# Merging and joining block inverses in one step, with decays and Gram matrices one step further ahead

## The chip, the cores and the metric

The kernel runs on one core of one Trainium2 chip. The metric is the device time of one execution in microseconds (us). TensorE (PE), VectorE (DVE), ScalarE (ACT) and GpSimd (POOL) compute, each working off its own list of instructions in order; SyncE (SP) issues the DMAs of this kernel, also in order.

## The reference

Three stages follow each other: a recurrent attention over 768 time steps for 4 batches and 8 heads with a state of 40x40, a feed-forward layer with a convolution of three taps, and a mixing layer with Fourier transforms, a norm and two matrices. The change touches the first:

```python
for t in range(S):
    kt, vt, rt = (k[:, :, t], v[:, :, t], r[:, :, t])
    wt, at, bt = (w[:, :, t], a[:, :, t], b[:, :, t])
    y[:, :, t] = np.einsum('bhd,bhde->bhe', rt, state)
    Sa = np.einsum('bhde,bhe->bhd', state, at)
    state_decay = state * wt[:, :, None, :] - np.einsum('bhd,bhe->bhde', Sa, bt)
    state = state_decay + np.einsum('bhd,bhe->bhde', vt, kt)
...
h = np.maximum(x @ w_in, 0.0)
...
gate = 1.0 / (1.0 + np.exp(-conv_out))
return (h * gate @ w_out).astype(np.float32)
```

## The kernel before, in words

The recurrence is done in 12 chunks of 64 time steps. Inside a chunk it is a triangular system, so that each chunk needs the inverse of a 64x64 triangular matrix per head and batch. `Attn.run` (L583 and on) counts steps n from 0 to 51; step n works on chunk n // 4 and batch n % 4, in stages: `stage_u` applies the inverse, `stage_h` (3 steps later, for the next chunk), `stage_s` and `stage_g` (1 step later), `stage_y` (2 steps later), `stage_sb` and `stage_o` (3 steps later). `stage_g` ends in one DVE product that writes the tile `gt` (L470); there is one in each step, so that the ends of two of them in a row bound a step on DVE.

Work is done ahead in `ahead` (L578). For a half chunk (two batches) `load_pre` (L146) loads `w`, `a` and `kb` and `decay` (L153) makes the decays: two scans on DVE (L161 and L165), and on POOL the products with `kb` (L176) and `a` (L168). This leads by LD = 17 steps. `gram` (L205) leads by LG = 15: matmuls of `abd` and `kb`, copies on ACT into `l0`, `l1` (tile `l`, L234 to L236) and `lk`.

Two chunks form a group (the first two chunks stand alone), and `inverse` (L312) inverts a group's diagonal blocks at once: a transpose of `l0` into A on DVE (L313), then 30 pairs of DVE instructions, a product (L333) and a sum (L336), each pair depending on the one before: the chain. POOL then clears a triangle (L338, L340), DVE makes three transposes (L343 into `t`, L346 twice into `tt`). The merge is a set of small matmuls on PE (`bp`), copied by ACT to `t` (L364); the join a second set (`mp`), copied to `tt` (L377). `stage_u` of the group's first chunk reads `tt`; the step in which it does so is the group's `end` (8, 16, 24, 32, 40 for the groups of two chunks).

The chain's instructions are given out at a rate over the steps between a group's start and its end (`rate`, L665 or so, in `run`), and `joins` (L516) issues the merge in step end - 2 and the join in step end - 1:

```python
for last, m in (("merge", v["end"] - 2), ("join", v["end"] - 1)):
    if v["last"] == last and n >= m:
```

A group starts when the Gram matrices of both its chunks have been issued (`na + LG >= 8 * g`), which is in step end - 7. A scheduler then puts the instructions of each engine into their final order. Between the steps runs the side work (`Moe.prep`): pieces of the later layers' weights are read as pairs of words and turned into floats by `unpack` (L766): ACT writes `pm` (L775) and the low words `py` (L776), DVE works on `pm` (L778, L780, L785), POOL adds `py` (L782), DVE and ACT split off a low part (L749, L752). The 33 last pieces are unpacked during the feed-forward layer, 64 unpackings in all with the one of the convolution's weights.

Of the kernel before, what the change touches and what calls it, by code (L numbers as in the profile page):

```python
# [10 lines left out]
F32 = mybir.dt.float32  # L11
# [13 lines left out]
P3 = HG * D  # L25
# [28 lines left out]
PC = 256  # L54
# [9 lines left out]
RI = 0.8  # L64
SIDE = 0.75
N1ST = 4
NA = 7
HL = 3
LG = 15
LD = 17  # L70
ST0 = 29
ST2 = 1
WARM = 4
# [25 lines left out]
class Attn:  # L99
# [53 lines left out]
    def decay(self, c, hb):  # L153
        nc, pre = self.nc, self.pre
        d = self.hf[c, hb]
        w, a, kb = d["w"], d["a"], d["kb"]

        wx = pre.tile([P3, 6, 66], F32, name="wx", tag="wx", bufs=11)
        vx = self.early.tile([P3, 6, 66], F32, name="vx", tag="vx", bufs=2)
        flat = [v.rearrange("p a b -> p (a b)") for v in (w, wx, vx)]  # L160
        nc.vector.tensor_tensor_scan(flat[2][:, ::-1], flat[0][:, ::-1], self.ends[:, ::-1], 0.0,  # L161
                                     op0=ALU.mult, op1=ALU.add)

        nc.vector.reciprocal(self.ends.rearrange("p (a b) -> p a b", b=66)[:, :, 0:1], vx[:, :, 1:2])
        nc.vector.tensor_tensor_scan(flat[1], flat[0], self.ends, 0.0, op0=ALU.mult, op1=ALU.add)  # L165
        nc.gpsimd.tensor_copy(wx[:, :, 65:66], vx[:, :, 1:2])
        e = nc.vector if c < 1 else nc.gpsimd
        e.tensor_tensor(a, a, wx[:, :, 0:C], op=ALU.mult)  # L168
        for h in range(HG):
            if c < 1:  # L170
                mul = nc.vector.tensor_scalar_mul if h == 2 else nc.scalar.mul
                v = mul(self.abd[hb][:, h], a, self.mdiag[:, D * h:D * h + 1])
                self.late = self.late if h == 2 else v
            else:
                nc.sync.dma_start(self.abd[hb][D * h:D * h + D, h], a[D * h:D * h + D])
        self.markp = nc.gpsimd.tensor_tensor(kb, kb, vx[:, :, 2:66].unsqueeze(2).to_broadcast([P3, 6, 2, C]), op=ALU.mult)  # L176
        d.update(wx=wx, vx=vx)
# [337 lines left out]

    def joins(self, live, n):  # L516
        for v in live:
            for last, m in (("merge", v["end"] - 2), ("join", v["end"] - 1)):
                if v["last"] == last and n >= m:
                    v["last"] = next(v["inv"], None)  # L520
                    yield
                    break

    def step(self, n, pre):
        def at(k):
            return divmod(n - k, B) if 0 <= n - k < B * NCH else (None, None)

# [15 lines left out]
        if c is not None:  # L546
            self.stage_g(c, b)
            if b % 2 and c + 1 < NCH:
                self.load_z(c + 1, b // 2)
            yield  # L550
        for _ in pre:
            yield
        c, b = at(3)
# [8 lines left out]
        if c is not None:  # L562
            self.stage_o(c, b)
            yield


    def in_range(self, flag):
# [10 lines left out]
    def ahead(self, n):  # L578
        m = n + LD
        if m % 2 == 0 and m < B * NCH:  # L580
# [4 lines left out]
            yield  # L585
        m = n + LG
        if m < B * NCH:
# [6 lines left out]
    def run(self, side):  # L594
# [24 lines left out]
        inv = self.inverse(0)  # L619
# [35 lines left out]
        live, g = [], 1  # L655
# [9 lines left out]
        for n in range(B * NCH + 4):  # L665
# [3 lines left out]
            while g <= NCH // 2 and na + LG >= 8 * g and len(live) < 2:  # L669
                end = 8 * g - 8 if g > 1 else 4  # L670
# [4 lines left out]
            pre = []  # L675
            for _ in range(1 + (n < NA)):
                if na <= n:
                    pre.append(self.ahead(na))
                    na += 1
            for _ in self.step(n, itertools.chain(self.joins(live, n), *pre)):  # L680
                sd += SIDE if n >= N1ST else 0.0
                while sd > 0:
                    with ExitStack() as st:
# [29 lines left out]
class Moe:  # L713
# [54 lines left out]
    def unpack(self, tp, raw, p, w):  # L768
        nc = self.nc

        def t(tag, dt):
            return tp.tile([128, PC], dt, name=tag, tag=tag, bufs=2)[:p, :w]
        lo, hi = raw[:, :, 0], raw[:, :, 1]
        m, y = t("pm", F32), t("py", I32)
        nc.scalar.activation(m, hi.bitcast(F32), AF.Abs)  # L775
# [3 lines left out]
        m = m.bitcast(I32)  # L779
# [630 lines left out]
```

## Time and profile before

| what | value |
|---|---|
| median of 3 runs | 1005.81 us (1003.6 to 1008.03) |
| the profiled execution | 1006.97 us |
| its span, first to last instruction | 1005.0 us |
| mean granted TensorE clock | 0.908 |
| stretch of the recurrence's steps 4 to 47, by the ends of `gt` | 119.54 to 503.36 us |

The profile gives the busy time of each engine, the waits (who stood idle, and whose instruction ended the wait), the busy times in chosen stretches, and the instructions in order of time. A wait by PE for a DVE instruction means that PE, which works in order, stood still with all that stands behind in its list. A busy time of DVE near the length of a stretch means that DVE sets the pace there. Share of busy time over the whole span says little, since the three stages have different limits.

### The profile page before, as it was taken

Reading aid. Unit: us, or ns where it says so; the run is one execution under the profiler, and the core shown is the slowest. Engines: PE = TensorE matmul, PEld = TensorE weight load, DVE = VectorE, ACT = ScalarE, POOL = GpSimd, SP = SyncE. Lnnn points to the kernel's source line nnn. Section 1 sums busy time; section 2 is a strip of 40 time slices with the busy share of each in tenths; the row PEclk is TensorE's granted clock in tenths of the full one; section 3 lists DMA queues with packets and bytes.
Section 4 is the critical chain, followed back from the end, with each engine's and each line's share of the span. In section 5 each row is a group of like instructions: output and inputs, shape, how many; then the busy total and the mean of one; then the engine's idle time right before and its main releaser. Section 6 shows DMA issues by size and latency. Waiting matters only on the chain. (4 is left out here: it accounts for less than half of the span.)

```text
span 1005.0 us, 21806 instructions
## 1 busy us (share of the span) xinstructions
PE 824.0 (82%) x8178; PEld 748.7 (75%) x8178; DVE 670.5 (67%) x1320; ACT 518.4 (52%) x1448; POOL 437.7 (44%) x507
## 2 busy tenths in 40 slices
PE   5548749747866868859699799998999999999997
PEld 3447638736766767849587577776879999999997
DVE  6994895994996894983169787978694444424321
ACT  4656638745865766535265566657464431222211
POOL 5455345653564553443157666765563112101000
PEclk8758768987997997978799999999999999999999
DMA  9623344662662752637545452212105000000000
GB/s 233 173 64 96 92 122 134 179 185 75 173 173 73 194 135 77 165 82 198 133 129 133 160 171 88 90 47 60 53 1 171 21 1 21 20 20 21 20 14 31
DMA packets 102989, 101.15 MB, mean 101 GB/s; under 512 B 47272, under 2 KB 89115, under 8 KB 102875
## 3 DMA queue, kind: packets, MB, share of 16 engines
q1 hardware_dynamic: 100907, 94.73, 33.5%
q0 software_dynamic: 1968, 4.93, 1.5%
q8 instruction: 67, 1.10, 0.5%
q14 instruction: 47, 0.39, 0.1%
HBM read 74.81 MB, written 20.76 MB: 95 GB/s over the span
## 5 line engine op out<-in xcount | busy, mean ns | idle before, releaser
L878 DVE SCALAR_TENSOR_TENSOR c<-h,cw,c 128x384 f32<-128x384 f32 x128 | 111.5, 875 | 21.5 <-ACT c L876 17.9
L1132 DVE SCALAR_TENSOR_TENSOR gl<-hp,gh 128x384 fp32r<-128x384 f32 x80 | 44.4, 556 | 111.3 <-ACT gh L1131 111.3
L895 PE MATMUL acc<-w_out_f,z 128*128 128x320 f32 x384 | 114.8, 436 | 4.7 <-POOL z L882 2.0
L1131 ACT ACTIVATE gh<-hp 128x384 fp32r<-128x384 f32 x80 | 39.2, 491 | 149.9 <-PE hp L701 149.7
L895 PEld LDWEIGHTS acc<-w_out_f,z 128*128 128x128 f32 x384 | 71.3, 190 | 28.2 <-POOL z L882 3.4
L701 PE MATMUL hp<-xh,w_in_h 128*128 128x386 f32 x192 | 76.1, 396 | 15.5 <-ACT h L869 15.5
L701 PE MATMUL hp<-uh,w_ch_h 128*128 128x384 f32 x240 | 82.3, 343 | 0.0
L701 PE MATMUL hp<-ul,w_ch_h 128*128 128x384 f32 x240 | 81.0, 338 | 0.0
L219 PE MATMUL gram<-abd,kb 120*128 120x192 f32 (+1 forms) x288 | 63.8, 371 | 16.9 <-DMA abd<-a 10.9
L1155 POOL DMA_INDIRECT out<-o,rows x12 | 11.8, 982 | 150.4 <-DVE o L1150 131.9
L457 POOL TENSOR_TENSOR st<-st,sm 120x360 f32<-120x360 f32 x40 | 43.5, 1087 | 70.8 <-DVE sm L456 47.8
L1145 PE MATMUL acc<-w_ch_h,gh 128*128 128x320 f32 x240 | 73.2, 312 | 0.0
L1145 PE MATMUL acc<-w_ch_l,gh 128*128 128x320 f32 x240 | 73.0, 309 | 0.0
L219 PEld LDWEIGHTS gram<-abd,kb 120*128 120x128 f32 x288 | 58.3, 235 | 19.0 <-issue 11.3
L388 PE MATMUL yp<-x,gt 128*64 128x40 f32 x768 | 63.6, 240 | 7.9 <-DVE gt L470 7.2
L333 DVE TENSOR_TENSOR tmp<-A 128x30 f32<-128x30 f32 (+9 forms) x150 | 68.1, 454 | 3.0
L388 PE MATMUL gp<-rbd,zt 120*128 120x192 f32 (+1 forms) x288 | 57.8, 341 | 13.4 <-DVE xo L509 6.0
L701 PE MATMUL hp<-xl,w_in_h 128*128 128x386 f32 x192 | 66.8, 348 | 0.0
L336 DVE TENSOR_TENSOR A<-A,tmp 128x30 f32<-128x30 f32 (+9 forms) x150 | 64.9, 433 | 2.6
L388 PE MATMUL bp<-t,l 32*32 32x32 f32 x768 | 21.2, 233 | 55.4 <-DVE t L343 50.8
L388 PEld LDWEIGHTS yp<-x,gt 128*64 128x64 f32 x768 | 58.5, 144 | 10.8 <-DVE gt L470 10.4
L879 ACT ACTIVATE c<-c 128x384 f32<-128x384 f32 x64 | 33.4, 521 | 61.0 <-DVE c L878 60.8
(225 smaller groups left out, 2610.9 us busy)
## 6 DMA issues: line engine op xcount, KB each, us to landing
kb<-in_kb SPq DMA_DIRECT2D x24, 360.0 KB
vbd<-in_vbd SPq DMA_DIRECT2D x24, 320.0 KB
xd<-xo SPq DMA_DIRECT2D x56, 90.0 KB
w<-in_w SPq DMA_DIRECT2D x24, 185.6 KB
a<-in_a SPq DMA_DIRECT2D x24, 180.0 KB
z<-in_zv SPq DMA_DIRECT2D x24, 180.0 KB
zt<-in_vt SPq DMA_DIRECT2D x24, 180.0 KB
rbd<-in_r SPq DMA_DIRECT2D x72, 60.0 KB
```

The lines of the kernel that those rows point to most:

```text
L219: nc.tensor.matmul(gp[:, 192 * gi:192 * gi + 64 * nh], d["kb"][:, bl * NG + gi].rearrange("p a b -> p (a b)"), abd[:, 0:nh, bl * NG + gi], ...
L333: nc.vector.tensor_tensor(tmp, A[:, s + 1:32, s:s + 1].to_broadcast([128, n, s]), A[:, s:s + 1, 0:s].to_broadcast([128, n, s]), op=ALU.mult)
L336: nc.vector.tensor_tensor(A[:, s + 1:32, 0:s], A[:, s + 1:32, 0:s], tmp, op=ALU.add)
L388: self.lastpe = op(*args, **kw)
L457: nc.gpsimd.tensor_tensor(self.st[b], self.st[b], t, op=ALU.add)
L701: nc.tensor.matmul(out, l, r, start=(j == 0), stop=(j == len(ops) - 1))
L878: nc.vector.scalar_tensor_tensor(c, h[:, j:HS + j], cw[:, f, j:j + 1], c, op0=ALU.mult, op1=ALU.add)
L879: nc.scalar.activation(c, c, AF.Sigmoid)
L895: nc.tensor.matmul(self.acc[t][:, 0:DM], z[:, ts], w[:, f], start=(f == 0), stop=(f == NF1 - 1))
L1131: self.mark = nc.scalar.activation(gh, hp[:, 0:HS], AF.Relu)
L1132: nc.vector.scalar_tensor_tensor(gl, hp[:, 0:HS], 0.0, gh.bitcast(F32), op0=ALU.max, op1=ALU.subtract)
L1145: nc.tensor.matmul(self.acc[t][:, 0:DM], l[:, ts], r, start=(f == 0 and j == 0), stop=(f == NF2 - 1 and j == 2))
```

## The change

NA, LG and LD go up by one: decays lead by 18 steps and Gram matrices by 16. The starting phase in which two calls of `ahead` are made in a step lasts 8 steps and not 7, so that the calls of the first 7 steps are the same as before. A group starts one step earlier against its end, and the rate falls with the longer stretch. Merge and join are both issued in the group's last step before use: the merge where joins stood, ahead of the work for later chunks, the join as the last work of the step. The decays `wx` get a twelfth buffer, and the low words `py` have one buffer in place of two. The 9 buffers of `a` stay.

```diff
-NA = 7
+NA = 8
 HL = 3
-LG = 15
-LD = 17
+LG = 16
+LD = 18
...
-        wx = pre.tile([P3, 6, 66], F32, name="wx", tag="wx", bufs=11)
+        wx = pre.tile([P3, 6, 66], F32, name="wx", tag="wx", bufs=12)
...
     def joins(self, live, n):
         for v in live:
-            for last, m in (("merge", v["end"] - 2), ("join", v["end"] - 1)):
-                if v["last"] == last and n >= m:
-                    v["last"] = next(v["inv"], None)
-                    yield
-                    break
+            if v["last"] in ("merge", "join") and n >= v["end"] - 1:
+                v["last"] = next(v["inv"], None)
+                yield
...
-    def step(self, n, pre):
+    def step(self, n, pre, live):
...
+        yield from self.joins(live, n)
         for _ in pre:
             yield
...
         if c is not None:
             self.stage_o(c, b)
             yield
+        yield from self.joins(live, n)
...
-            for _ in self.step(n, itertools.chain(self.joins(live, n), *pre)):
+            for _ in self.step(n, itertools.chain(*pre), live):
...
-            return tp.tile([128, PC], dt, name=tag, tag=tag, bufs=2)[:p, :w]
+            return tp.tile([128, PC], dt, name=tag, tag=tag, bufs=1 if tag == "py" else 2)[:p, :w]
```

What this does to the lists of PE and DVE is shown for the group whose end is step 16. First PE before, in step 14, after the matmuls of `stage_g` (`gp`); `bp` is the merge, `gram`, `xp` and `ss` are work for later chunks and for the next state:

```order
L388 MATMUL gp<-rbd_91,zt 128x192 x2
L388 MATMUL gp<-rbd_91,zt 128x128
L388 MATMUL bp<-t_2793,l_1423 32x32 x64
L219 MATMUL gram<-abd_89,kb 128x192 x2
L219 MATMUL gram<-abd_89,kb 128x128
L255 MATMUL xp<-ident,kb 128x120 x3
L388 MATMUL ss<-ident,st_103 120x120 x3
```

The join (`mp`) stood at the same place in step 15. Now the merge stands in step 15, with the join behind the last transposes of that step and just ahead of the `u` that reads its result:

```order
L388 MATMUL gp<-rbd_92,zt 128x192 x2
L388 MATMUL gp<-rbd_92,zt 128x128
L388 MATMUL bp<-t_2806,l_1423 32x32 x64
L219 MATMUL gram<-abd_90,kb 128x192 x2
L219 MATMUL gram<-abd_90,kb 128x128
L255 MATMUL xp<-ident,kb 128x120 x3
L388 MATMUL ss<-ident,st_100 120x120 x3
L388 MATMUL up<-ident,z_111 120x64 x3
L388 MATMUL yt<-ident,ys_108 120x64 x3
L388 MATMUL mp<-tt_132,t_2806 32x32 x64
L388 MATMUL u<-hbd_96,tt_132 64x80
```

So the merge moved by one step, and one step of other work no longer lies between merge and join. Second, DVE before, from the chain's last sum in step 14 to the next `gt`; seven pairs of the chain stand in the same step ahead of these rows:

```order
L336 TENSOR_TENSOR A<-A,tmp 128x30
L343 STREAM_TRANSPOSE t_2793<-A 128x32x32
L346 STREAM_TRANSPOSE tt_132<-A 128x32x32 x2
L509 TENSOR_TENSOR xo<-yt,wx 120x192
L165 SCALAR_TENSOR_TENSOR wx<-w,ends 120x396
L164 RECIPROCAL ends<-vx 120x6
L161 SCALAR_TENSOR_TENSOR vx<-w,ends 120x396
L452 TENSOR_TENSOR sm_112<-sp,mdiag 120x240
L456 TENSOR_TENSOR sm_112<-sp,mdiag 80x80
L470 TENSOR_TENSOR gt<-gp,mlt 128x512
```

Now the three transposes of this group stand two `gt` ahead of the merge's step, and after the `gt` of the merge's step DVE has the start of the next group's chain:

```order
L470 TENSOR_TENSOR gt<-gp,mlt 128x512
L785 SCALAR_TENSOR_TENSOR pm<-raw,pm 128x256
L752 TENSOR_TENSOR wl<-pm,wh 128x256
L509 TENSOR_TENSOR xo<-yt,wx 120x192
L313 STREAM_TRANSPOSE A<-l_2191 128x1024
L333 TENSOR_TENSOR tmp<-A 128x30
L336 TENSOR_TENSOR A<-A,tmp 128x30
L778 TENSOR_SCALAR pm<-pm 128x256
L333 TENSOR_TENSOR tmp<-A 128x58
L780 TENSOR_SCALAR pm<-pm 128x256
L336 TENSOR_TENSOR A<-A,tmp 128x29x2
L333 TENSOR_TENSOR tmp<-A 128x84
```

Nine pairs of the chain stand there ahead of the next `gt`, where before the same place had no chain instruction. The groups with ends 24 and 32 are moved alike. For the group with end 40, PE's list has merge and join in the same places as before, and only DVE's differs.

## Rows read from the trace of the kernel before

**Rows 1.** The page's first part: busy us, share of the span, instructions.
```profile
PE 824.0 (82%) x8178; PEld 748.7 (75%) x8178; DVE 670.5 (67%) x1320; ACT 518.4 (52%) x1448; POOL 437.7 (44%) x507
```

**Rows 2.** Waits from 66 to 476 us: who waited for whom: us, times, longest.
```profile
ACT t L364 <- PE bp L388: 64.6, 10, 14.8
PE bp L388 <- DVE t L343: 50.8, 5, 12.4
...
DVE t L343 <- POOL A L340: 7.9, 5, 1.6
```

**Rows 3.** Windows bounded by ends of `gt`: length, busy us (instructions), clock, DMA.
```profile
119.54:171.73 52.19, 35.94 (x558) 33.38 (x558) 39.20 (x73) 33.04 (x103) 26.87 (x29) 0.74 0.42 120
171.73:253.62 81.89, 56.07 (x846) 50.92 (x845) 66.26 (x135) 50.91 (x163) 43.43 (x47) 0.85 0.53 150
253.62:329.58 75.96, 56.62 (x850) 51.72 (x849) 64.11 (x132) 49.54 (x161) 44.33 (x49) 0.87 0.49 136
329.58:401.39 71.81, 54.84 (x851) 50.01 (x850) 57.38 (x126) 47.99 (x156) 35.17 (x44) 0.88 0.50 136
401.39:460.45 59.06, 44.95 (x794) 40.73 (x794) 46.96 (x116) 27.74 (x80) 22.08 (x27) 0.86 0.44 115
sum 340.91, PE 248.42 PEld 226.76 DVE 273.90 ACT 209.23 POOL 171.87; mean PE 49.68 PEld 45.35 DVE 54.78 ACT 41.85 POOL 34.37
```

**Rows 4.** The same for three single steps: PE, PEld, DVE, ACT, POOL.
```profile
164.78:171.73 6.95, 5.81 (x77) 5.18 (x75) 3.42 (x9) 6.72 (x21) 4.34 (x6) 1.00 0.61 183
220.89:244.78 23.89, 14.41 (x335) 13.66 (x336) 15.21 (x29) 7.92 (x23) 9.74 (x12) 0.62 0.29 76
244.78:253.62 8.84, 6.28 (x79) 5.65 (x78) 3.09 (x10) 7.83 (x22) 2.92 (x5) 1.00 0.57 166
```

**Rows 5.** Four stretches full of chain (188.51, 261.06, 338.22, 408.59 on), summed.
```profile
sum 141.66, PE 104.41 PEld 93.48 DVE 139.29 ACT 89.58 POOL 82.61; mean PE 26.10 PEld 23.37 DVE 34.82 ACT 22.39 POOL 20.65
```

**Rows 6.** Timeline of PE in step 14: start, us, what, idle before it.
```profile
216.89 1.11 PE L388 MATMUL gp<-rbd,zt 120*128 120x192 f32 x6 [2.64 <-DVE xo L509]
230.37 3.62 PE L388 MATMUL bp<-t,l 32*32 32x32 f32 x128 [12.37 <-DVE t L343]
233.92 2.08 PE L219 MATMUL gram<-abd,kb 120*128 120x192 f32 x6
```

**Rows 7.** Timeline of DVE in the same step, after the chain.
```profile
228.38 1.93 DVE L343 STREAM_TRANSPOSE t<-A 128x1024 f32<-128x1024 f32 x1 [1.59 <-POOL A L340]
230.20 3.65 DVE L346 STREAM_TRANSPOSE tt<-A 128x1024 f32<-128x1024 f32 x2
237.79 0.36 DVE L509 TENSOR_TENSOR xo<-yt,wx 120x192 f32<-120x192 f32 x1 [3.94 <-PE yt L388]
```

**Rows 8.** Timeline of ACT in the same step: merge's copies, then the Gram matrix's.
```profile
232.33 1.17 ACT L364 COPY t<-bp 32x512 f32<-32x512 f32 x2 [11.86 <-PE bp L388]
234.04 1.16 ACT L364 COPY t<-bp 32x512 f32<-32x512 f32 x2 [0.54 <-PE bp L388]
...
237.20 0.27 ACT L236 ACTIVATE l<-gram 32x128 f32<-32x128 f32 x1
```

**Rows 9.** Timeline around 208.6 us: chain instructions of DVE, product of POOL.
```profile
208.50 0.39 DVE L333 TENSOR_TENSOR tmp<-A 128x234 f32<-128x234 f32 x1
208.92 1.02 DVE L336 TENSOR_TENSOR A<-A,tmp 128x234 f32<-128x234 f32 x1
...
208.59 1.09 POOL L168 TENSOR_TENSOR a<-a,wx 120x384 f32<-120x384 f32 x1
```

**Rows 10.** Timeline around 560 us: a low-word tile written, the one before it read.
```profile
558.71 0.43 ACT L776 ACTIVATE py<-raw 128x256 int32<-128x256 uint32 x1
...
561.76 0.82 POOL L782 TENSOR_TENSOR pm<-pm,py 128x256 int32<-128x256 int32 x1
```

**Rows 11.** Timeline: a load of `a` issued, and the product that reads it.
```profile
328.56 0.41 SPq L151 DMA_DIRECT2D a<-in_a  x1
...
334.35 1.12 POOL L168 TENSOR_TENSOR a<-a,wx 120x384 f32<-120x384 f32 x1
```

## The prediction

> **What bounds the kernel now.** I read the busy times first, and they decide nothing: PE leads with 82% of the span and DVE has 67% [rows 1], but that averages three stages. The change touches only the recurrence, so I read the waits there next. PE waited five times for the transpose at the end of an inverse, 50.8 us together, at most 12.4 us [rows 2]: once for each group of two chunks. The timeline of one such wait shows how. PE finished `gp` at 218.0, and the merge could start only at 230.4 [rows 6], since DVE was still at the chain and its transposes [rows 7]. During the wait nothing new comes to DVE from PE; afterwards it is DVE's turn to stand, 3.94 us for the next `yt` [rows 7]. So the two engines stall each other in turn in that step, which took 23.89 us with 15.21 us of work on DVE [rows 4].
>
> The windows say what there is to gain. From 119.54 to 460.45 us, five windows of which each holds one such stall, DVE was busy for 273.9 of 340.9 us [rows 3]: 67.0 us idle. In stretches full of chain it is idle for only 2.4 of 141.7 us, or 1.7% [rows 5]. So DVE bounds those steps, and its idle time sits in the merge's step and in the steps behind it that have no chain: 3.5 us in the step that ended at 171.73, 5.8 us in the one that ended at 253.62 [rows 4].
>
> **The change part by part.** No DVE instruction is added or taken away in the recurrence. What can change is DVE's 67.0 us of idle time. I therefore count what idle time the new order leaves.
>
> (a) Steps with chain keep the 1.7%: of 274 us, 4.6 us.
>
> (b) The merge comes one step later and the chain one step earlier, so the transposes are done before PE asks, and there is a step without chain ahead of the merge's in the three middle groups. It has a scan, `xo`, `gt` and side work. The nearest rows are the chainless steps before, 6.95 us long with 3.42 busy [rows 4]. The new step holds a scan or two more, so I take 2 us idle each, 6 us in all; ends 0 and 10.5 us (3 times 3.5).
>
> (c) The next chain's first transpose reads the last Gram matrix of its group, which now stands behind the merge on PE and behind the merge's copies on ACT. Before, at half clock, it was 7.1 us from the merge's start at 230.37 to the end of that Gram matrix's last copy at 237.47 [rows 6, 8]. In the changed order PE has not stood still before the merge, as it had at a granted clock of 0.62 in that step against 1.00 in the steps beside it [rows 4]. At full clock I take half of the merge's 3.62 us and of the Gram matmuls' 2.08 us [rows 6] off, 2.8 us, and get 4.3 us. DVE has `gt`, two side products and `xo` to do in that time, some 2.3 us (`xo` alone is 0.36 [rows 7], the others about twice that). So it waits 2 us for each of three groups. For the group that starts in step 8, PE's list has two sets of Gram matmuls behind the merge, and the transposes of the group before are still in the same step. I take the full 7.1 us there. Sum 13 us; ends 0 (the copies come early) and 28 us (four times 7.1).
>
> (d) The transposes wait for POOL to clear the triangle, 7.9 us over five groups [rows 2]. Three small DVE products now stand in between; I take 3 us, ends 0 and 8.
>
> (e) The last window has no next chain to fill it. Its last two steps have about 2.5 us of DVE work each. I take 4.4 us for the first, as PE's steps with few Gram matmuls go, and 11 us for the second (merge, join, their eight copies of 0.58 us [rows 8], and a step's own matmuls in a row). Idle: 10.5 us; ends 6 and 15.
>
> Sum of (a) to (e): 37.1 us, and 67.0 - 37.1 = 29.9 us less.
>
> (f) Closer packing puts more of POOL's work beside DVE's. A chain sum on 234 elements took 1.02 us with a POOL product beside it, and its partner of the same size 0.39 us just before [rows 9]. POOL is busy for 171.9 of the 340.9 us [rows 3], 50%; in 313 us it would be 55%. Five hundredths of DVE's 274 us are 14 us with POOL beside them that had none. Most DVE work isn't hit as hard as this pair, so I take a fifth, 3 us; ends 0 and 14.
>
> (g) One buffer for `py` makes ACT wait until POOL has read the piece before. In the trace the write came ahead of the end of the read 7 times in 63, by 11.9 us together, at most 3.9 us: 558.71 against 562.58 [rows 10]. Most of that is in the feed-forward stage, where ACT is idle for a third of the time. I take 1 us on the path; ends 0 and 12.
>
> (h) At no cost: `wx`'s buffer (it covers the longer lead), LD with the first steps (the calls of the first seven steps are the same). Merge and join in one step put both sets of copies, 4.6 us of ACT, into that step; its DVE list has the next chain's nine pairs to work on meanwhile, and that covers them. Where the cover is gone, in (e), they are in the sum. SP's list keeps its order around the weights' loads at the end of the recurrence, so I leave the stretch from 460.45 to 503.36 as it is, and all that follows it moves up.
>
> So 29.9 - 3 - 1 = 25.9 us less. From the profiled execution's 1006.97 us that is 981.1; the runs' median lies 1.2 us lower, at 1005.81, and the forecast with it: **980 us**, 2.6% less. No change and noise can't be told apart within about 0.5%, 5 us.
>
> **The rivals.** *More comes off.* If the next chain's transpose never waits and nothing else fills the gap, (c) and (d) vanish and (b) goes to its lower end: 22 us more, 958 us. For it speaks that the Gram copies take only 1.6 us on ACT (six of 0.27 [rows 8]) and the scheduler may have put them well; against it that they stand behind the merge in ACT's list.
>
> *POOL eats half.* The mechanism is (f) at its upper end: every microsecond of added overlap costs DVE a microsecond, 14 us, in place of 3. That gives 991 us. For it: the pair of [rows 9]; against it: DVE reached 98% busy with POOL at 82.61 of 141.66 us beside it [rows 5], and these durations already have the overlap in them. The Trainium skill, "SBUF — State Buffer", section "Who interferes with whom", says that a DVE instruction with two inputs in SBUF and a GpSimd instruction that reads SBUF block each other for the whole instruction. By that rule the sum would hold the 14 us, and 991 us would be the forecast; the trace agrees for single pairs (1.02 against 0.39 us), and no run here shows how often it strikes.
>
> *The loads of `a` come too late: slower.* Nine buffers hold 18 steps and the lead is now 18, so a load can be issued only after the `stage_h` of its own step has read the buffer, while the product on POOL wants to run a step earlier than before. 13 loads are made inside the steps. The shortest time from issue to product was 5.8 us [rows 11]; if POOL had to stand that long each time with the state's update (L457, L458) queued behind, and PE after it, 13 times 5.8 is 75 us, less the 26 gained: 49 us slower, 1055 us. It decides from 2 us each time (26 / 13) that gets through to PE. Against it: POOL's product waits for the scan on DVE anyway, the state is read more than a step after its update, and no wait of PE for POOL's state is among the long ones [rows 2].
>
> *The change doesn't do what it says*, as where a scheduler keeps the old order: excluded, since the lists show merge and join moved in four of five groups. For the fifth only DVE's list moved, but its chain ends sooner there, too.
>
> **How the numbers follow.** Forecast, 16 to 34 us less: 0.52. More: 0.17. POOL or another wait that halves the gain, 5 to 16 us less: 0.14. Gains and losses that cancel within 5 us: 0.09. Late loads, or a wait that I don't see, slower: 0.08. So faster 0.83, same 0.09, slower 0.08. The range reaches from 957, a little past the first rival, to 1001, where the cases that leave less than the bound of no change begin: about 0.08 is left out above, and some 0.1 below.
>
> **What would show it.** In the changed profile PE's five waits for L343 should shrink from 50.8 us to under 10; the windows between the same ends of `gt` should sum to about 314 us with DVE still busy for 274 to 280; a new wait of L313 for L236 should show, about 13 us; the last window should end on a chainless step of about 11 us. The sum is wrong if DVE's busy time grows by over 10 us, if PE waits for POOL's state, if SP stands at the load of `a`, or if the stretch after the last window changes its length.

## The result and the profile after

The changed kernel takes **978.33 us** (median of 4 runs, 976.56 to 979.85) against 1006.62 us for the kernel before in the same comparison: a ratio of 0.9719, 95% interval 0.9696 to 0.9741. The profiled execution took 977.45 us, with a span of 975.5 us and a mean granted clock of 0.925. The forecast was 980 us.

The busy times on the changed kernel's page, to be held against [rows 1]:

```profile
span 975.5 us, 21804 instructions
PE 818.7 (84%) x8178; PEld 745.1 (76%) x8178; DVE 668.3 (69%) x1320; ACT 519.7 (53%) x1448; POOL 433.2 (44%) x507
```

Busy times differ by at most 5.3 us on any engine, while the span is 29.5 us shorter. So work did not become less; engines stand less. The windows between the same ends of `gt` say where (start and end, length, busy us of PE, PEld, DVE, ACT, POOL, granted clock, DMA share, GB/s); they answer to [rows 3]:

```profile
120.55:178.76 58.21, 35.06 (x587) 32.64 (x587) 50.74 (x96) 39.64 (x125) 30.00 (x31) 0.87 0.43 121
178.76:251.48 72.72, 56.55 (x848) 51.73 (x848) 67.46 (x133) 50.28 (x159) 43.24 (x47) 0.89 0.61 164
251.48:319.43 67.95, 53.73 (x823) 49.16 (x824) 60.33 (x127) 47.33 (x153) 39.46 (x46) 0.90 0.56 156
319.43:384.92 65.49, 51.88 (x867) 47.85 (x865) 59.02 (x131) 48.07 (x153) 33.40 (x43) 0.95 0.55 147
384.92:435.92 51.00, 42.93 (x766) 39.03 (x768) 37.26 (x95) 23.96 (x67) 20.28 (x25) 0.90 0.44 118
sum 315.37, PE 240.16 PEld 220.41 DVE 274.80 ACT 209.28 POOL 166.37; mean PE 48.03 PEld 44.08 DVE 54.96 ACT 41.86 POOL 33.27
```

The five windows are 25.5 us shorter, and DVE's busy time in them is what it was, 274.8 us. Its idle time fell from 67.0 to 40.6 us. Read the first and the last window together: the first is 6.0 us *longer* than before, but DVE has 11.5 us more to do in it, since the chains now start a step earlier; the last has 9.7 us less. By idle time the five windows changed by -5.5, -10.4, -4.2, -8.0 and +1.6 us.

The remaining 4 us of the span: the windows begin 1.0 us later, the stretch from the last window to the `gt` of step 47 takes 39.9 us and not 42.9, and what follows 499.7 us and not 501.6.

Waits in the five windows (who stood, for whom, us, times, longest); first two of the changed kernel's PE, where [rows 2] had 50.8 us for the first of them (the second took 7.2 us before):

```profile
PE bp L388 <- DVE t L343: 10.1, 1, 10.1
PE yp L388 <- DVE gt L470: 18.4, 11, 5.1
```

Then DVE's waits of the kernel before over its five windows:

```profile
DVE xo L509 <- PE yt L388: 22.1, 7, 6.1
DVE sm L452 <- PE sp L388: 14.8, 5, 7.0
DVE t L343 <- POOL A L340: 7.9, 5, 1.6
...
DVE A L313 <- ACT l L236: 0.5, 1, 0.5
```

and of the changed kernel:

```profile
DVE A L313 <- ACT l L236: 12.0, 4, 6.3
DVE sm L452 <- PE sp L388: 8.0, 5, 4.8
DVE xo L509 <- PE yt L388: 4.8, 3, 2.1
DVE pm L785 <- POOL pm L782: 4.7, 3, 2.1
DVE vx L161 <- POOL st L458: 3.0, 2, 1.5
```

Four of PE's five stalls are gone, and with them DVE's return waits for PE's results (`yt` and `sp`, 36.9 us before, 12.8 now). Two waits took their place: the next chain's first transpose for the Gram matrix's copies, 12.0 us, and a weight piece for POOL, 4.7 us. DVE no longer waits for POOL's triangle.

One merge on PE's timeline, for the group whose end is step 16 (start, us, engine, line, what, out<-in, count, idle before it); it answers to [rows 6]:

```profile
230.38 1.08 PE L388 MATMUL gp<-rbd,zt 120*128 120x192 f32 x6
231.38 2.36 PE L388 MATMUL bp<-t,l 32*32 32x32 f32 x128
233.67 1.14 PE L219 MATMUL gram<-abd,kb 120*128 120x192 f32 x6
```

The transposes stand on DVE's timeline ten microseconds ahead, and after the merge's `gt` the next chain begins:

```profile
219.61 2.12 DVE L343 STREAM_TRANSPOSE t<-A 128x1024 f32<-128x1024 f32 x1
221.60 3.71 DVE L346 STREAM_TRANSPOSE tt<-A 128x1024 f32<-128x1024 f32 x2
...
236.68 0.35 DVE L509 TENSOR_TENSOR xo<-yt,wx 120x192 f32<-120x192 f32 x1
239.01 1.96 DVE L313 STREAM_TRANSPOSE A<-l 128x1024 f32<-128x1024 f32 x1 [1.98 <-ACT l L236]
```

PE runs from `gp` into `bp` with no stop. The one group that kept its stall ends in step 8:

```profile
155.15 3.63 PE L388 MATMUL bp<-t,l 32*32 32x32 f32 x128 [10.08 <-DVE t L343]
164.98 1.96 DVE L313 STREAM_TRANSPOSE A<-l 128x1024 f32<-128x1024 f32 x1 [6.34 <-ACT l L236]
```

The same 128 small matmuls take 2.36 us in the one and 3.63 us in the other. The granted clock over them (the third number from the end, columns as in the windows above) was 1.00 in the one and 0.50 in the other, behind a stand of 10.08 us:

```profile
231.38:233.74 2.36, 2.36 (x130) 2.30 (x129) 0.85 (x3) 2.30 (x8) 2.36 (x5) 1.00 0.40 113
155.15:158.78 3.63, 3.63 (x129) 3.57 (x129) 3.49 (x2) 1.16 (x2) 0.02 (x1) 0.50 0.02 5
```

Last, the steps that the prediction priced: the three without chain ahead of a merge, then the last two of the fifth window (columns as in the windows above):

```profile
227.48:235.54 8.06, 7.26 (x195) 6.76 (x191) 6.48 (x11) 6.08 (x18) 7.86 (x9) 1.00 0.58 154
...
297.97:305.21 7.24, 6.37 (x185) 6.04 (x182) 5.63 (x12) 2.44 (x8) 6.85 (x8) 1.00 0.49 131
365.05:369.70 4.65, 4.07 (x109) 3.78 (x107) 3.90 (x9) 2.17 (x7) 4.02 (x6) 1.00 0.69 175
420.40:426.79 6.39, 6.34 (x80) 5.95 (x82) 2.26 (x7) 1.54 (x6) 3.72 (x5) 0.53 0.20 58
426.79:435.92 9.13, 8.93 (x308) 8.22 (x302) 1.89 (x8) 6.99 (x16) 1.15 (x3) 1.00 0.19 50
```

### The profile page after: what moved, and what is told of

Same layout as the page of the kernel before. It is cut to its first block, busy times and chain, and to the rows that moved or that the text cites. A ratio compares the mean times of both kernels' runs of the same rounds, so it can differ in the third digit from the quotient of the medians.

```text
span 975.5 us, 21804 instructions
## 1 busy us (share of the span) xinstructions
PE 818.7 (84%) x8178; PEld 745.1 (76%) x8178; DVE 668.3 (69%) x1320; ACT 519.7 (53%) x1448; POOL 433.2 (44%) x507
## 5 line engine op out<-in xcount | busy, mean ns | idle before, releaser
L878 DVE SCALAR_TENSOR_TENSOR c<-h,cw,c 128x384 f32<-128x384 f32 x128 | 101.6, 798 | 17.3 <-ACT c L876 15.4
L219 PE MATMUL gram<-abd,kb 120*128 120x192 f32 (+1 forms) x288 | 59.5, 353 | 17.8 <-DMA a<-in_a 11.2
L333 DVE TENSOR_TENSOR tmp<-A 128x30 f32<-128x30 f32 (+9 forms) x150 | 70.1, 467 | 3.1
L219 PEld LDWEIGHTS gram<-abd,kb 120*128 120x128 f32 x288 | 55.1, 224 | 19.4 <-issue 11.6
L336 DVE TENSOR_TENSOR A<-A,tmp 128x30 f32<-128x30 f32 (+9 forms) x150 | 67.3, 449 | 2.9
L782 POOL TENSOR_TENSOR pm<-pm,py 128x160 int32<-128x160 int32 (+2 forms) x64 | 44.4, 693 | 41.2 <-DVE pm L780 22.3
L1145 PE MATMUL acc<-w_ch_h,gl 128*128 128x320 f32 x240 | 61.4, 309 | 0.0
```

The costliest lines, as they stand in the source:

```text
L219: nc.tensor.matmul(gp[:, 192 * gi:192 * gi + 64 * nh], d["kb"][:, bl * NG + gi].rearrange("p a b -> p (a b)"), abd[:, 0:nh, bl * NG + gi], ...
L333: nc.vector.tensor_tensor(tmp, A[:, s + 1:32, s:s + 1].to_broadcast([128, n, s]), A[:, s:s + 1, 0:s].to_broadcast([128, n, s]), op=ALU.mult)
L336: nc.vector.tensor_tensor(A[:, s + 1:32, 0:s], A[:, s + 1:32, 0:s], tmp, op=ALU.add)
L782: nc.gpsimd.tensor_tensor(m, m, y, op=ALU.add)
L878: nc.vector.scalar_tensor_tensor(c, h[:, j:HS + j], cw[:, f, j:j + 1], c, op0=ALU.mult, op1=ALU.add)
L1145: nc.tensor.matmul(self.acc[t][:, 0:DM], l[:, ts], r, start=(f == 0 and j == 0), stop=(f == NF2 - 1 and j == 2))
```

## The experiments

The theory: PE and DVE stall each other in turn in the step of a merge, and the change gains because the chain's transposes end a step ahead. Its rivals: the gain comes from one half of the change alone; it comes from less work on DVE in that step; the loads of `a` or the single `py` buffer take part of it away. Windows and waits below come from one profiled execution of each kernel, while the runs of one kernel lie 1 to 12 us apart, so that differences of one or two us between windows decide nothing.

**The joins alone.** Merge and join in the last step before use, with the old leads and buffers (the calls in `step` and `run` as in the change):

```diff
-            for last, m in (("merge", v["end"] - 2), ("join", v["end"] - 1)):
-                if v["last"] == last and n >= m:
+            if v["last"] in ("merge", "join") and n >= v["end"] - 1:
```

> Only the merge and join move (both into step end - 1); leads of 17 and 15, 11 buffers of wx and 2 of py stay. Theory (the time follows the idle time of VectorE in the five windows up to 460 us): the merge no longer falls into the middle of the chain's last pairs, but the next group's chain starts only a step after the use, so the merge's step still has nothing for VectorE to do. Per group some 9 us idle stay of the 13.4 (67.0 / 5): about 20 us less than before, 986 us, between 980 and 993. Rival A (the late merge is the whole gain, and the leads only feed it): 978 us, as with the full change, within 3. Rival B (the leads are the whole gain): 1006, as before.

Measured: 999.24 us (998.03 to 1001.04), ratio 0.9928 (0.9902 to 0.9954). PE's stalls, from the waits:

```profile
PE bp L388 <- DVE t L343: 41.9, 5, 11.6
```

and the sum of its five windows:

```profile
sum 340.59, PE 250.53 PEld 229.38 DVE 278.17 ACT 209.02 POOL 172.36; mean PE 50.11 PEld 45.88 DVE 55.63 ACT 41.80 POOL 34.47
```

All five stalls are still there, and the windows are as long as before: DVE idles 4.6 us less in them and has 4.3 us more to do. The 7 us came from outside them: 40.1 us after the last window and not 42.9, and 495.6 us and not 501.6 in what follows, with windows that begin 1.7 us later.

**The leads alone.** LG 16, LD 18, NA 8, `wx` 12, `py` 1; merge and join as before.

```diff
-NA = 7
+NA = 8
...
-LG = 15
-LD = 17
+LG = 16
+LD = 18
```

> Only the leads move (18 and 16, 8 doubled steps, 12 buffers of wx, 1 of py); the merge stays in step end - 2 and the join in end - 1. Theory (VectorE's idle time): the next chain fills the step behind the merge, but TensorE still comes to the merge while VectorE has 2 to 4 pairs and three transposes left, so TensorE's wait for L343 stays at some 5 us a group and VectorE is idle for some 9 us behind it: about 20 us less, 985 us, between 979 and 993. The two halves together are then less than their sum (28 us with both). Rival A (only the merge's place counts): 1006. Rival B (leads alone): 978. Rival C (halves are independent and add up): e1's gain and this one's sum to 28 us.

Measured: 993.65 us (993.04 to 994.12), ratio 0.9871 (0.9839 to 0.9902). The windows sum to 330.3 us, and all five stalls are there again:

```profile
PE bp L388 <- DVE t L343: 39.6, 5, 14.0
```

So both expectations fell: neither half gives 20 us. The halves give 8 and 14 us of the whole time, and both together 28. In the windows they give 0.3 and 10.6 us, and both together 25.5. Either half adds a step between chain and merge, and in neither did the scheduler's list put the transposes ahead of the merge's step, but for the group that ends in step 32: there they stand late in the step before, and PE waits only 3.0 and 2.0 us. With both halves it did so for four groups.

**The merge behind the Gram matrices.** To take away the 12.0 us wait of L313:

```diff
-        yield from self.joins(live, n)
         for _ in pre:
             yield
+        yield from self.joins(live, n)
```

> The changed kernel with one line moved: the merge is issued behind the step's work ahead (Gram matmuls and their transposes), not ahead of it. The next chain's first transpose then has its Gram copies before the merge's copies on ScalarE. Theory, term (c): VectorE's wait of L313 for L236, 14.2 us with the change, falls under 4 us, and about 8 us of it comes off the time: 970 us. Rival (the wait only changes its place: the join now follows the merge too closely, TensorE waits for the merge's copies, and the step is as long): 978 within 3 us, with TensorE's wait of the join for L364 up from 6.1 us to 12 or more.

Measured: 980.49 us (979.38 to 984.08), ratio 0.9754 (0.9717 to 0.979), no gain over the change. Within the windows the wait of L313 is gone, but DVE stands elsewhere, by its waits there:

```profile
DVE sm L452 <- PE sp L388: 18.9, 9, 6.7
DVE t L343 <- POOL A L340: 7.8, 3, 5.3
```

and the windows sum to 3 us more than the changed kernel's:

```profile
sum 318.34, PE 251.24 PEld 229.91 DVE 270.15 ACT 209.68 POOL 163.99; mean PE 50.25 PEld 45.98 DVE 54.03 ACT 41.94 POOL 32.80
```

The scheduler drew more of the next chain into the merge's step (15 to 18 pairs where there were 7 to 11), so that three or four steps per group were left without chain ahead of it, where there were two. The rival of the expectation had the time right, within 3 us of 978, but not the reason: PE waited 2.8 us in the windows for the merge's copies ahead of the join. The wait was 12.0 us, and what replaced it 18.7 (10.9 more for `sp`, 7.8 for the triangle). A wait's length is not what its removal gives.

**A tenth buffer for `a`** (and `wx` back to 11 for space):

```diff
-        for key, shape, n in (("w", [P3, 6, 66], 3), ("a", [P3, 6, C], 9), ("kb", [P3, 6, 2, C], 3)):
+        for key, shape, n in (("w", [P3, 6, 66], 3), ("a", [P3, 6, C], 10), ("kb", [P3, 6, 2, C], 3)):
```

> The changed kernel with 10 buffers of a in place of 9, and 11 of wx in place of 12 to make room. Theory: GpSimd's wait of L168 for the load of a (16.8 us in five waits with the change) goes to under 3 us, but the state's update behind it has a step of slack, so the time stays within 3 us of 978; wx's eleventh buffer costs nothing since the writer and the last reader of a buffer are both on VectorE. Rival (the late loads of a reach TensorE): 6 us or more faster, 972 or less. Second rival (wx needs its twelfth buffer): slower by 3 us or more.

Measured: 982.94 us (981.57 to 983.55), ratio 0.9765 (0.9733 to 0.9798). In the changed kernel POOL did stand for late loads within the windows:

```profile
POOL a L168 <- DMA a<-in_a: 10.1, 4, 4.8
```

Here that wait is gone altogether and the windows sum to 314.5 us, 0.9 less. So the late loads were real, and taking them away gave no more than a microsecond in the windows. The time is 4.6 us longer, more than expected, because the stretches behind the windows are: 42.7 and 503.0 us against 39.9 and 499.7. That has the size of the second rival (`wx` needs its twelfth buffer); but the kernel with eleven `wx` and two `py` buffers, below, takes 979.5 us, so `wx` alone doesn't explain it. The cause is open.

**Two more steps of lead, joins as before.** Leads of 19 and 17, NA 9, from the kernel with the leads alone:

```diff
-NA = 8
+NA = 9
...
-LG = 16
-LD = 18
+LG = 17
+LD = 19
```

> The leads go up by two steps (decays 19, Gram matrices 17, starting phase 9 steps), and merge and join stay where they stood before, in the steps end - 2 and end - 1. So a chain has seven steps before its merge, as in the change, without the change's two places. Theory (what counts is how many steps a chain has ahead of its merge, seven of them, wherever merge and join stand): PE's waits for L343 fall to under 12 us, the five windows to 312 to 322 us, the time to 977 to 985 us. Rival (merge and join have to stand in one step): the waits stay over 35 us and the windows over 328 us, as with either half alone; 990 us or more. If late loads of the a buffers cost time after all, it shows here first, since the lead is one step longer over the same nine buffers: POOL's wait for them grows beyond the 16.8 us of the changed kernel, and if half of that growth got through to PE the time would be 985 to 995 us with PE's waits for L343 gone all the same.

Measured: 988.91 us (987.06 to 991.47), ratio 0.9827 (0.9798 to 0.9856), between the two. Its first three windows:

```profile
120.50:178.03 57.53, 35.32 (x582) 32.73 (x582) 44.24 (x79) 38.68 (x123) 28.02 (x30) 0.85 0.44 119
178.03:260.20 82.17, 58.28 (x837) 53.31 (x838) 75.32 (x156) 51.84 (x164) 42.29 (x47) 0.83 0.53 147
260.20:328.31 68.11, 54.64 (x875) 48.70 (x873) 60.98 (x131) 52.44 (x171) 40.76 (x47) 0.97 0.57 155
```

and what is left of PE's stalls:

```profile
PE bp L388 <- DVE t L343: 23.8, 2, 13.7
```

The number of steps alone doesn't decide. For the groups that end in 8 and 16 the list still has the transposes in the merge's step, and PE stands 13.7 and 10.2 us. For the others the transposes stand ahead, PE doesn't wait, and the third and fourth windows (68.1 and 65.2) are as long as those of the changed kernel, with merge and join at their old places. POOL stood 18.3 us for late loads of `a` in the five windows, and the third and fourth are no longer for it. The second window has to be read with care. It is as long as before (82.2), but not for PE's stall of 10.2 us: DVE idles only 6.9 us in it, near the changed kernel's 5.3, and has 75.3 us to do, since 40 pairs of chain stand there where the changed kernel has 29. Right behind this merge DVE finds the next chain, and so PE's stall costs it little.

**Two buffers for `py`** in the changed kernel (`wx` 11):

```diff
-            return tp.tile([128, PC], dt, name=tag, tag=tag, bufs=1 if tag == "py" else 2)[:p, :w]
+            return tp.tile([128, PC], dt, name=tag, tag=tag, bufs=2)[:p, :w]
```

> The changed kernel with two buffers for py and eleven for wx, as before. Theory (one buffer of py costs about 1 us, term (g), and the twelfth wx buffer gives nothing): 975 to 980 us, and the stretch after step 47 within 3 us of the changed kernel's 499.7 us. Rival (the upper end of (g)): 12 us less, 966 us, all of it in the stretch after step 47. Second rival (the longer lead needs the twelfth wx): the five windows grow by over 5 us from 315.4 us, with DVE's scans L165 waiting for the products of POOL that read wx.

Measured: 979.5 us (979.09 to 980.64), ratio 0.9738 (0.9717 to 0.9759); windows 313.7 us, stretch after step 47 501.7 us, 2.0 us more. Both buffers together count for nothing in the whole time; the kernel was not run with one of them alone.

**No side work between the recurrence's steps**, in the kernel before:

```diff
-SIDE = 0.75
+SIDE = 0.0
```

> The kernel before with SIDE at 0: no piece of the later layers' weights is unpacked between the recurrence's steps once the starting phase is over; that work moves behind the recurrence. DVE's side work in the five windows before was about 55 us of its 273.9 us. Theory (the order of the lists makes the stall: the chain's end and its transposes stand in the merge's step, whatever else DVE has to do): PE's waits for L343 stay over 35 us, and DVE idles 50 us or more of windows that sum to 270 to 290 us. Rival (the stall comes from a DVE that has too much to do, so that the chain comes late): the waits fall under 15 us and the windows to 235 to 255 us. The stretch after step 47 grows by tens of us under both, so that the whole time says little.

Measured in a single run: 1009.48 us. The expectation was wrong on where the work goes: the scheduler drew it forward, the windows start at 148.3 us and not 119.5, and the stretch after step 47 kept its 501.0 us. PE's stalls:

```profile
PE bp L388 <- DVE t L343: 35.9, 5, 10.7
```

In the windows DVE has 27.6 us less to do:

```profile
sum 320.24, PE 247.54 PEld 227.15 DVE 246.32 ACT 195.94 POOL 153.58; mean PE 49.51 PEld 45.43 DVE 49.26 ACT 39.19 POOL 30.72
```

The five stalls stay and DVE idles 73.9 us, more than before. The stall is one of order, not of too much work on DVE.

**A rate of 0.65, in four kernels.** RI is the rate at which a chain's instructions are given out. At 0.65 the merge can be issued only in step end - 1, and the scheduler's lists come out with other places for the transposes. First the changed kernel with that rate, and with the Gram matrices ahead of the merge in step 7:

```diff
-RI = 0.8
+RI = 0.65
...
-        yield from self.joins(live, n)
+        if n > 7:
+            yield from self.joins(live, n)
         for _ in pre:
             yield
+        if n <= 7:
+            yield from self.joins(live, n)
```

> The changed kernel with a rate of 0.65 in place of 0.8, so that the second group's chain is issued sooner against its end and its transposes stand in step 6 on DVE, and with the merge of that group behind the Gram matrices of step 7 and not ahead of them. Theory (the one wait that is left, 10.1 us in step 7, is the same stall as the four that went): it goes, and the first window shrinks from 58.2 us by 4 to 9 us; the time is 969 to 975 us. Rival (the starting phase is bound by DVE, 50.7 of 58.2 us, and the wait's time is only moved to the steps beside it): the first window stays within 3 us of 58.2 us and the time within 976 to 981 us.

Measured: **968.26 us** (966.41 to 969.85), ratio 0.9625 (0.96 to 0.9651), the fastest of all by its median, and clear of the changed kernel's interval. The stall in step 7 is gone (2.5 us are left, in the last group). Its first window, and the sum of the five:

```profile
120.42:171.56 51.14, 37.52 (x599) 33.88 (x596) 45.76 (x94) 41.70 (x131) 29.47 (x32) 0.87 0.52 142
...
sum 305.19, PE 244.50 PEld 224.06 DVE 266.83 ACT 211.36 POOL 164.83; mean PE 48.90 PEld 44.81 DVE 53.37 ACT 42.27 POOL 32.97
```

The first window lost 7.1 us. Of that 5.0 us are work that DVE no longer has in it, and only 2.1 us are idle time. Chain work was drawn ahead of the windows, into steps where DVE had stood: five pairs more stand there, it is busy for 8.0 us less in the five windows than in the changed kernel, and their start, 120.42 us, is no later for it. (The expectation says that the chain is issued sooner; the rate is lower, and it is the list that has the transposes sooner.)

Then the leads alone with that rate, the joins' code as before the change:

```diff
-RI = 0.8
+RI = 0.65
```

> The leads alone (18 and 16, starting phase 8, wx 12, py 1; joins as before the change) with a rate of 0.65 in place of 0.8. At this rate a chain's instructions are given out more slowly, so that the merge can be issued only in the step end - 1, though its place in the code is the old one, and in the lists of instructions the transposes of four groups stand a step ahead of their merge and those of the group that ends in step 8 early in the merge's own step. Theory (PE's stall is there exactly where a list has the transposes late in the merge's step; the code for merge and join and the place they are written at don't matter beyond that): PE's waits for L343 fall from the 39.6 us of the leads alone to under 10, the windows from 330.3 to between 303 and 317 us, the time from 993.65 to between 965 and 980 us. Rival (the change's own places of merge and join are needed): the windows stay over 325 us and the time over 988 us.

Measured: 972.34 us (964.34 to 972.56), ratio 0.9637 (0.9589 to 0.9684). PE never waits for L343, and the windows sum to

```profile
sum 309.15, PE 248.59 PEld 226.80 DVE 263.00 ACT 211.47 POOL 167.08; mean PE 49.72 PEld 45.36 DVE 52.60 ACT 42.29 POOL 33.42
```

The leads alone had all five stalls and took 993.65 us; one number, the rate, makes 21 us of difference with the same instructions. Not all of that is stall: in the windows DVE idles 8.5 us less and is busy for 12.7 us less. Of these, 3.2 us moved ahead of the windows; over the whole execution the same 1320 instructions kept DVE busy for 672.6 us in the one kernel and 660.7 in the other, and what made them shorter was not tried. The change's code for the joins is not needed for a gain of this size.

The changed kernel with the rate alone:

> The changed kernel with the rate of 0.65 alone, its Gram matrices behind the merge in step 7 as in the change. Theory (what the best version so far gained came from the transposes of the group that ends in step 8, which the rate brings to the front of the merge's step): the first window stays 5 to 9 us under the changed kernel's 58.2 us and the time is 966 to 972 us. Rival (the Gram matrices of step 7 ahead of the merge made it): the first window is within 3 us of 58.2 us, PE waits 5 us or more there, and the time is 975 to 980 us.

Measured: 977.36 us (976.32 to 978.03), ratio 0.9711 (0.9686 to 0.9737). No merge waits in the five windows. The first of them:

```profile
120.91:170.16 49.25, 37.20 (x602) 34.00 (x600) 42.84 (x85) 41.15 (x131) 29.41 (x32) 0.86 0.52 148
```

It is 9.0 us shorter than the changed kernel's, but DVE has 7.9 us less to do in it, of which 5.0 us went ahead of the windows; its idle time fell by 1.1 us. And the time is that of the changed kernel: the second to fifth windows and the stretches behind them gave 1.1, 2.8, 2.4, 0.7, 0.5 and 1.5 us back. So removing the last stall was worth 1 us, of DVE's idle time there as of the whole, and neither expectation has that case. Nor does it explain the 968.26 us of the kernel with Gram matrices ahead of the merge in step 7: that one is longer than this in its first and third window, by 1.9 and 2.6 us, and shorter in its second, fourth and fifth and in what follows step 47, by 5.4, 4.6, 2.6 and 2.7 us, though its edit touches only the steps up to 7. Why is open.

And the kernel before with the rate alone:

> The kernel before with the rate of 0.65 alone, leads of 17 and 15. In its lists the merges move into the step end - 1, and the transposes of the groups stand in the same step as their merge, or in the one just before. Theory (a slower rate has no worth of its own; with these leads the chain cannot end ahead of the merge's step): PE's waits for L343 stay over 30 us, the windows within 331 to 345 us, the time within 993 to 1008 us. Rival (the rate by itself makes the gain of 10 us seen with the changed leads): the waits fall under 15 us, the windows under 325 us and the time under 988 us.

Measured: 990.44 us (984.23 to 996.53), ratio 0.9839 (0.9779 to 0.9899), 3 us below the expected range by the median, with runs 12 us apart. The theory that a slower rate has no worth of its own doesn't hold: it gave 16 us. PE's stalls:

```profile
PE bp L388 <- DVE t L343: 31.2, 4, 9.5
```

and the first window:

```profile
120.38:164.11 43.73, 33.40 (x569) 30.73 (x568) 32.36 (x62) 36.05 (x113) 26.10 (x29) 0.88 0.53 148
```

Four stalls stay. The one that went is again the one whose transposes moved forward, and its window is the one that shrank most, by 8.5 us. But 6.8 of them are work that DVE no longer has in it, and DVE idles 11.4 us there, against 13.0 before with a stall of 10.3 us on PE: the two steps around the merge hold no chain, so that DVE stands all the same. The stretch between the last window and step 47 took 33.2 us, 9.7 less than before; what made it shorter was not tried.

## Why the prediction was right, point by point

| kernel | median us | PE for L343, us (times) | five windows | DVE busy in them | DVE idle in them | to step 47 | after it |
|---|---|---|---|---|---|---|---|
| before, no side work (one run) | 1009.5 | 35.9 (5) | 320.2 | 246.3 | 73.9 | 37.9 | 501.0 |
| before | 1006.6 | 50.8 (5) | 340.9 | 273.9 | 67.0 | 42.9 | 501.6 |
| joins alone | 999.2 | 41.9 (5) | 340.6 | 278.2 | 62.4 | 40.1 | 495.6 |
| leads alone | 993.7 | 39.6 (5) | 330.3 | 275.7 | 54.6 | 39.6 | 501.3 |
| before, rate 0.65 | 990.4 | 31.2 (4) | 333.6 | 269.9 | 63.7 | 33.2 | 502.7 |
| leads 19 and 17, old joins | 988.9 | 23.8 (2) | 325.4 | 271.6 | 53.8 | 40.6 | 501.6 |
| change, ten `a`, eleven `wx` | 982.9 | 7.8 (1) | 314.5 | 276.1 | 38.4 | 42.7 | 503.0 |
| merge behind Gram | 980.5 | 13.7 (1) | 318.3 | 270.1 | 48.2 | 38.9 | 500.5 |
| change, two `py`, eleven `wx` | 979.5 | 7.9 (1) | 313.7 | 276.1 | 37.5 | 43.0 | 501.7 |
| **the change** | 978.3 | 10.1 (1) | 315.4 | 274.8 | 40.6 | 39.9 | 499.7 |
| change, rate 0.65 | 977.4 | 0 | 313.3 | 265.2 | 48.1 | 40.4 | 501.2 |
| leads alone, rate 0.65 | 972.3 | 0 | 309.2 | 263.0 | 46.1 | 37.5 | 502.9 |
| change, rate 0.65, Gram first in step 7 | 968.3 | 2.5 (1) | 305.2 | 266.8 | 38.4 | 41.1 | 498.5 |

(Windows and the columns beside them from each profiled execution, by the ends of `gt` of steps 3, 7, 15, 23, 31, 39 and 47.)

*What bounds it.* Right for the change: four of five stalls went, DVE's work in the windows stayed (273.9 and 274.8 us), and its idle time fell by 26.4 us, which is the gain in the windows. Over all rows PE's stall is a looser guide. The joins alone have 9 us less waiting and no shorter windows, and the two kernels at the rate of 0.65 that have no stall idle DVE for 46 and 48 us, more than the change with one; their windows are shorter since DVE has 10 to 12 us less to do in them. Two windows above show why. A stall costs little where DVE has the next chain at hand (10.2 us of stall, 6.9 us of idle time), and its absence gains little where DVE has none (no stall, 11.4 us of idle time). I read this as that the gain takes both, transposes ahead of the merge and the next chain behind it, and that the halves of the change don't add up for that; no run was made to show it by itself.

*The sum in the windows.* Forecast 314 us with 274 to 280 us of DVE, measured 315.4 with 274.8. But the idle time that was left has other parts than the working gave:

- (b) light steps ahead of the merge: 6 us forecast, 3.9 measured (1.58, 1.61 and 0.75), nearly all of it DVE standing for POOL (1.51 us twice for L458, 0.71 for L782);
- (c) L313 for the Gram copies: 13 forecast, 12.0 measured, and in the right places: 6.34 us in the group that starts in step 8 (7.1 forecast), where the merge still ran at a granted clock of 0.50 and took 3.63 us, then 1.98, 3.42 and 0.23 (2 each forecast). The forecast halved the merge's 3.62 us for the full clock; at a granted clock of 1.00 it took 2.36 us, not 1.81;
- (d) POOL's triangle: 3 forecast, no wait measured;
- (e) the end of the last window: 10.5 forecast, 11.4 measured, as 4.1 and 7.2 in steps of 6.4 and 9.1 us, where I had taken 4.4 and 11;
- (a) what leaks in steps with chain: 4.6 forecast, and 13.3 measured, all that is left of 40.6. This is the term that was mis-sized. I took the 1.7% from stretches in which DVE is the only bound. Of the 13.3 us, 6.2 lie in the steps of the first four merges, beside the wait of L313, 2.7 of them for `yt`, which no term had; the other 7.1 lie in the 27 remaining steps, 2.1 of them in one wait for POOL's part of a weight piece (L782; the rest of its 4.7 us falls into (b) and (e)).

The errors nearly cancel: 37.1 us forecast, 40.6 measured. That the sum came out within 4 us is in part luck.

*(f) POOL beside DVE.* Forecast 3 us. The 272 chain instructions in the windows took 125.8 us after and 121.9 before, 3.9 more; DVE's other work took 3.0 less, so that its total rose by 0.9. The rival's 14 us did not come. Its premise came only in half: POOL was busy for 53% of the windows, not 55%, so that by its own reckoning it would have been 6.5 us.

*(g) and (h).* One `py` and twelve `wx` buffers, or two and eleven: no difference in the whole time. The slower rival had its mechanism. POOL stood 10.1 us at late loads of `a` within the windows, and SyncE, whose standing at the load of `a` the prediction named as a sign that the sum is wrong, stood there for the matmuls of `stage_h` that read the buffer (its waits in the windows, before and then after):

```profile
SPq L151 <- PE hu L388: 1.7, 1, 1.7
SPq L151 <- PE hu L388: 15.0, 8, 6.8
```

14.3 of the 15.0 us are loads of `a`. It hardly got through to the windows: with the tenth buffer they are 0.9 us shorter.

*What failed.* The sentence that the stretch after 460.45 us stays as it is. It lost 3.0 us to step 47 and 1.9 behind it, 4.9 of the 29.5 us, and the windows began 1.0 us later. Without that, the result would have been some 4 us higher, still within the range. In the steps 44 and 45 ACT stands for a DMA (`xf` from `xd`), 12.0 us before and 9.5 after, which has the size of the 3.0 us; this was not tried. The experiments moved these two stretches by up to 9.7 and 6.0 us against the kernel before, with edits that change nothing there but order and buffers.

*PE's waits under 10 us.* They came out at 10.1. I had priced the transposes that stay in the merge's step for the first group as DVE's wait alone, in (c). PE's stall of 10 us was left, too; the kernels with the lower rate show that it can go, and the changed kernel at that rate that its going gains 1 us.

## What to carry to other kernels

When two engines that work in order wait for each other in turn, count the idle time of the busier one, and look in the final lists of instructions for whether the producer stands ahead of the consumer's step. That told the stalls apart in every kernel here: waits of 5 to 14 us where the transposes stand in the merge's step, of 2 to 3 us where they stand late in the step before, none where they stand earlier; the code's own constants did not tell it. Compare windows with the busy time in them: a window can become 9 us shorter because work left it, with 1 us less of idle time. Parts of such a change don't add up: with either half the list still had the producer late, so that each gave a fraction. Before believing a few us from such an edit, compare the stretches that it should not touch; here they moved by several us on their own.

## What the runs showed of the hardware

How a POOL product falls on the chain is all or nothing for one instruction. In the changed kernel, first on DVE's timeline and then on POOL's (columns as in the timelines above):

```profile
242.14 0.24 DVE L333 TENSOR_TENSOR tmp<-A 128x84 f32<-128x84 f32 x1
242.42 1.78 DVE L336 TENSOR_TENSOR A<-A,tmp 128x84 f32<-128x84 f32 x1
...
314.77 0.25 DVE L336 TENSOR_TENSOR A<-A,tmp 128x84 f32<-128x84 f32 x1
```

```profile
242.41 1.69 POOL L176 TENSOR_TENSOR kb<-kb,vx 120x768 f32<-120x768 f32 x1 [1.86 <-DVE tmp L333]
```

The same sum takes 0.25 us at 314.77 and 1.78 us at 242.42, when POOL's product started in the same instant: DVE's instruction ends just after POOL's does. The Trainium skill, "SBUF — State Buffer", section "Who interferes with whom", says that whoever issues first holds the shared ports for its whole instruction, and these rows agree. So does the count over the five windows of the changed kernel. Of the chain's 272 instructions 149 ran with no POOL instruction beside them and 42 started ahead of one: none of these took over 0.15 us more than the shortest of its line and shape. 81 started after a POOL instruction that was still running: 66 of them took over 0.15 us more, and each of the 66 ended 0.05 to 0.27 us after it. In the kernel before it is 63 of 87, and again none of the others. I had not expected that the price goes by the chain instructions that are struck in this way: 63 became 66, and the chain's 272 instructions took 3% longer.
